# A fused attention and soft mixture of experts on one core: the dispatch softmax's second part one unit later, and the last batch's sums kept in x's unused third

## The chip, the cores and the metric

One core of a Trainium2 chip. The metric is the device time of one execution in microseconds (us); lower is better. The engines are TensorE (PE, its weight loads PEld), VectorE (DVE), ScalarE (ACT), GpSimd (POOL) and SyncE (SP), which issues all of this kernel's transfers.

## The reference

The input are q, k and v of 8 batches, 12 heads, 448 tokens and 64 columns, a matrix phi of 768 x 32, and the weights of 8 experts, w1 (768 x 1024 each) and w2 (1024 x 768 each), all fp32.

```
scores = q @ k.T / sqrt(64) - log(448)
attn   = sigmoid(scores)
x      = attn @ v                       # 3584 tokens x 768, heads side by side
logits = x @ phi                        # 3584 x 32 slots
d      = softmax of logits over the 3584 tokens (+ 1e-9 under the line)
slots  = d.T @ x                        # 32 x 768, 4 per expert
out_e  = relu(slots_e @ w1_e) @ w2_e    # for each of the 8 experts
c      = softmax of logits over the 32 slots (+ 1e-9)
result = c @ out                        # 3584 x 768
```

## The kernel before, in words

**Attention.** The heads are taken in pairs: 6 pairs per batch, 48 in all, each with its tokens in a free dimension of 448. The keys of a pair come in units of 128; the last 64 keys of two pairs share a unit, so two pairs make 7 units, a batch 21 and the whole 168 (`seq`). A unit (p, c) has two halves. `score` (L133) multiplies keys and queries into a PSUM tile `sc`, and a sigmoid on ScalarE (L137) writes the unit's buffer `att`, one of three in rotation. `weigh` (L157) multiplies that with v into `av`; it runs two units later (`LAG` = 2), so TensorE alternates between scoring unit i and weighing unit i - 2. Tile `av0` belongs to even pairs and `av1` to odd ones. The unit that two pairs share (c = 3) writes both.

After the third unit of a pair, `evac_a` (L160, VectorE) copies one half of the pair's `av` to x; after the shared unit, for an even pair, `evac_b` (L164) adds the other half. The weighing of the shared unit writes `av0` too, and it waits until `evac_a` has read it.

x is kept in `xr`, three thirds of three pairs each. A batch uses two of them, the next batch the third and the first, and so on; batch 7, the last, uses the thirds 2 and 0.

**The dispatch softmax, batch by batch.** While batch b + 1 is scored and weighed, the softmax over tokens of batch b is taken up, with a running maximum and a running sum per slot. Its parts are put into the attention's loop by three tables, `early`, `middle` and `late`, whose keys are places in that loop (i); with g the last unit of batch b, place g + n + LAG is the one at which unit g + n is weighed. In `late` what stands there follows the unit's weighing and its `evac_a` or `evac_b`.

- g + 2: `logits_job` (L173 on TensorE, then `softmax_a`: maximum and difference on VectorE), `softmax_b` (two sigmoids on ScalarE, L201 and L202, whose quotient is the exponential), then `turn` (L167, a transpose of one pair's x) and `softmax_c` (VectorE: reciprocal L207, product L208, transpose L209, sum L211 or L214, running sum L215, and the logits' transpose L217).
- g + 3 is the third unit of the next batch's first pair, so `evac_a` stands there; g + 4 is the shared unit, with `evac_b` and two turns.
- g + 5: `spread`, which SP issues: the weights go to DRAM (`zd`, L221) and come back in four copies (`dr`, L224); and two turns. g + 7: the last turn.
- g + 10: `slot_job`: the slot sums on TensorE (`slot_mm`, L246), added up in `acc` on VectorE (L261, L263).

The engines' orders are as written (`manual_schedule` for TensorE, SP, VectorE and ScalarE), each a strict sequence.

**The last batch** is not followed by attention. `last_job` does its softmax at once, on TensorE, VectorE and ScalarE, and its slot sums; L307 adds `acc`, scaled, to them in four instructions and writes `total`, 128 x 768, and L314 multiplies that into `sT`, the slots' input, on which the experts depend.

**Weights.** w1 and w2 are cut into 128 units of 384 KB. 56 go to the tiles `wa` during the attention. Of 11 further tiles `wb` the memory is that of the attention's pools `ldq`, `ldv`, `at` (where `att` is) and `xp` (where `xr` is), in this order; their loads (`load_unit`, L85) are issued after `last_job`, one after the other on SP, and each waits until what lay in its place is done with. The remaining 61 units follow in the ring of `wa` and `wb`, each when its tile's unit has been used. The experts run with w1 (L429) and then, for each half of the columns, with w2 (L528). After each half 16 output blocks are computed (L510, copied by L511) and written (L513), through the same ring and the same SP queue; those of the first half are computed within the second half's w2 steps.

Of the kernel before, what the change touches and what calls it, by code (L numbers as in the profile page):

```python
# [9 lines left out]
F32 = mybir.dt.float32  # L10
# [7 lines left out]
DM, NSLOT, E, SPE, F = 768, 32, 8, 4, 1024  # L18
P = 128
NFK = 3  # L20
LAG = 2
W_STEPS = 140
NPR = H // 2
NKC = DM // P
# [17 lines left out]
def soft_moe_attention(ctx: ExitStack, tc: tile.TileContext, qk, v, vl, phi, w1, w2, cst, out):  # L42
# [48 lines left out]
    with ExitStack() as actx:  # L91
        ldq = actx.enter_context(tc.tile_pool(name="ldq", bufs=3))
        ldv = actx.enter_context(tc.tile_pool(name="ldv", bufs=1))
        at = actx.enter_context(tc.tile_pool(name="at", bufs=3))
# [5 lines left out]
        xr = xp.tile([P, 3, 3, S], F32, name="xr")  # L100
# [4 lines left out]
        def x_of(p):  # L105
            b, hp = divmod(p, NPR)
            return xr[:, (2 * b + hp // 3) % 3, hp % 3, :]
# [58 lines left out]
        def turn(p):  # L166
            nc.vector.transpose(x_of(p), x_of(p))  # L167
# [9 lines left out]
        def logits_job(b):  # L177
            lg = ps_sc.tile([P, 2, 512], F32, name="sc")[:, 0, :]
            logits(lg, b, range(NPR))
            nc.vector.tensor_copy(lgs[0:96, :], lg[0:96, 0:P])  # L180
            nc.vector.tensor_copy(lgs[96:128, 0:64], lg[96:128, 0:64])
            softmax_a(b)
# [15 lines left out]
        def softmax_b(b):  # L198
            zt, pe = dts[b][:, 0, :], dts[b][:, 1, :]
            n = P if b == 0 else P + 1  # L200
            nc.scalar.activation(pe[:, 0:n], zt[:, 0:n], AF.Sigmoid)  # L201
            nc.scalar.activation(zt[:, 0:n], zt[:, 0:n], AF.Sigmoid, scale=-1.0)  # L202

        def softmax_c(b):
            zt, pe = dts[b][:, 0, :], dts[b][:, 1, :]
            n = P if b == 0 else P + 1
            nc.vector.reciprocal(zt[:, 0:n], zt[:, 0:n])  # L207
            nc.vector.tensor_tensor(out=pe[:, 0:n], in0=pe[:, 0:n], in1=zt[:, 0:n], op=ALU.mult)  # L208
            nc.vector.transpose(zt[:, 0:P], pe[:, 0:P])  # L209
            if b == 0:  # L210
                nc.vector.tensor_reduce(out=mz[:, 1:2], in_=pe[:, 0:P], axis=AX.X, op=ALU.add)  # L211
            else:
                zb = small.tile([P, 1], F32, name="zb")
                nc.vector.tensor_reduce(out=zb[:], in_=pe[:, 0:P], axis=AX.X, op=ALU.add)  # L214
                nc.vector.scalar_tensor_tensor(  # L215
                    out=mz[:, 1:2], in0=mz[:, 1:2], scalar=pe[:, P:P + 1], in1=zb[:], op0=ALU.mult, op1=ALU.add)
            nc.vector.transpose(lt_all[:, b, :], lgs[:])  # L217

        def spread(b):
            flat = bounce.tile([P, P], F32, name="zd")  # L220
            nc.sync.dma_start(flat[:], dts[b][:, 0, 0:P])  # L221
            drs[b] = xp.tile([P, 4, NBK * BLK], F32, name="dr")
            for a in range(4):
                nc.sync.dma_start(drs[b][32 * a:32 * a + 32, :, :], flat[:].rearrange("(j i) n -> i j n", j=4))  # L224
# [31 lines left out]
        def slot_job(b):  # L256
            sl = slot_mm(b)
            for g in range(2):
                part = sl[g][:, :, 0:NPR * BLK]
                if b == 0:  # L260
                    nc.vector.tensor_copy(acc_of(g), part)  # L261
                else:
                    nc.vector.scalar_tensor_tensor(  # L263
                        out=acc_of(g), in0=acc_of(g), scalar=dts[b][:, 1, P:P + 1], in1=part,
                        op0=ALU.mult, op1=ALU.add)

        def last_job(b, lgt):
# [33 lines left out]
            nc.vector.tensor_tensor(out=cw[:, 2:3], in0=m1[:, 1:2], in1=pa[:, P:P + 1], op=ALU.subtract)  # L301
            nc.scalar.activation(cw[:, 3:4], cw[:, 2:3], AF.Exp)
            nc.vector.tensor_scalar(sw, sel4, cw[:, 3:4], None, op0=ALU.mult)
            total = at.tile([P, DM], F32, name="att")
            by_block = total[:].rearrange("p (k a n) -> p k a n", k=NKC, a=4)
            for a in range(4):
                nc.vector.scalar_tensor_tensor(  # L307
                    out=by_block[:, :, a, :], scalar=cw[:, 1:2],
# [37 lines left out]
        for r in range(NP // 2):  # L346
            p = 2 * r
            seq += [(p, c) for c in range(NFK + 1)] + [(p + 1, c) for c in range(NFK)]
        per_b = len(seq) // B
        early, middle, late = {}, {}, {}  # L350
        for b in range(B - 1):
            g = (b + 1) * per_b - 1
            early[g + 2 + LAG] = [lambda b=b: logits_job(b)]
            middle[g + 2 + LAG] = [lambda b=b: softmax_b(b)]
            late[g + 2 + LAG] = [lambda b=b: turn(b * NPR), lambda b=b: softmax_c(b)]
            late[g + 4 + LAG] = [lambda b=b: turn(b * NPR + 1), lambda b=b: turn(b * NPR + 2)]
            late[g + 5 + LAG] = [lambda b=b: spread(b), lambda b=b: turn(b * NPR + 3), lambda b=b: turn(b * NPR + 4)]
            late[g + 7 + LAG] = [lambda b=b: turn(b * NPR + 5)]
            late[g + 10 + LAG] = [lambda b=b: slot_job(b)]

        for i in range(len(seq) + LAG):
# [20 lines left out]
            if i >= LAG:  # L382
                u = seq[i - LAG]
                weigh(u)
                p, c = u
# [13 lines left out]
        logits(lgt[:, 0, :], B - 1, [NPR - 1])  # L399
        turn(NP - 4)  # L400
        finish = last_job(B - 1, lgt)

    state["wpb"] = ctx.enter_context(tc.tile_pool(name="wpb", bufs=1, reuse_waits="tile"))
# [113 lines left out]
    for hf in range(2):  # L517
        po = ps_o.tile([P, 512], F32, name="po")
        n = 0
# [67 lines left out]
```

## Time and profile before

| | |
|---|---|
| median of 3 runs | 425.53 us (423.01 to 427.61) |
| the profiled execution | 426.35 us, of which the span from first to last instruction 424.5 us |
| busy, share of the span | PE 89%, DVE 39%, ACT 49%, POOL 1% |
| transfers | 97.64 MB, mean 230 GB/s |
| mean granted TensorE clock | 0.955 |

In the profile's rows L133 is the line of the kernel; `att<-sc` names the tile written and those read; a bracket at a row's end is the idle time of that engine just before it and what ended the idle time. `SPq` is SP's queue: its rows show the issue of a transfer, not the transfer. In the list of waits stand the total in us, the number of waits and the longest. Under `windows` the columns are each engine's busy time with its instructions, then TensorE's clock, the share of the DMA engines' time, and GB/s.

### The profile page before, as it was taken

What the parts mean: (1) busy time and instruction counts of PE and PEld (TensorE: products, weight loads), DVE (VectorE), ACT (ScalarE), POOL (GpSimd) and SP (SyncE); (2) the same over time, 40 slices, a digit from 0 to 9 for tenths busy, and PEclk for the clock granted to TensorE, in tenths of its full rate; (3) what the DMA queues carried; (4) which work ended last, traced back from release to release, by engine and by line L of the source; (5) the groups of instructions that cost most, each with busy time, mean ns of one, the idle gap of its engine ahead of it and who ended that gap; (6) DMA issues with size and microseconds to landing.
All of it is one profiled execution on the core that took longest, in us unless ns stands there. A gap on an engine that the chain in (4) does not pass through costs nothing.

```text
span 424.5 us, 11237 instructions
## 1 busy us (share of the span) xinstructions
PE 377.5 (89%) x4794; PEld 170.1 (40%) x4794; DVE 164.2 (39%) x383; ACT 206.0 (49%) x274; POOL 2.4 (1%) x12
## 2 busy tenths in 40 slices
PE   8999899989989998998999899899879968889730
PEld 5333343434334343433434343344355433334410
DVE  0222632453263236226423622542534653144430
ACT  4666546655645655564565556555400223433430
POOL 0000000000000000000000000000010000000000
PEclk9999999999999999999999999999968998969885
DMA  6667467558736755874665565252309999999987
GB/s 232 222 226 242 149 210 258 188 146 277 233 129 205 255 176 179 258 247 159 196 227 200 192 217 180 84 144 83 112 13 349 399 400 402 401 401 394 301 282 229
DMA packets 48770, 97.64 MB, mean 230 GB/s; under 512 B 5072, under 2 KB 26192, under 8 KB 48720
## 3 DMA queue, kind: packets, MB, share of 16 engines
q1 hardware_dynamic: 48720, 96.92, 67.0%
q8 instruction: 38, 0.62, 0.6%
q14 instruction: 12, 0.10, 0.1%
HBM read 85.43 MB, written 11.47 MB: 228 GB/s over the span
## 4 chain that ended last, share of the span: by engine, by line
PE 77%; DVE 10%; issue 4%; ACT 3%; DMA 1%; DVEq 0%; ACTq 0%
PE av L157 28%; PE sc L133 28%; PE po L528 5%; PE sc L173 3%; PE av L246 2%; PE sc L246 2%; PE ph L510 2%; PE ph L429 2%; DVE t L207 2%; PE pt L446 1%; DVE xr L160 1%; DVE tmp L442 1%; DMA out_dram<-wa 1%; PE pt L484 1%; PE pt L510 1%
## 5 line engine op out<-in xcount | busy, mean ns | idle before, releaser
L137 ACT ACTIVATE att<-sc,nbias 128x896 f32<-128x896 f32 x168 | 169.1, 1007 | 126.8 <-PE sc L133 126.8
L133 PE MATMUL sc<-qkt 64*64 64x448 f32 x1344 | 158.1, 541 | 0.2 <-ACT att L137 0.2
L157 PE MATMUL av<-att,v 64*64 64x448 f32 x1152 | 134.0, 536 | 0.0
L160 DVE COPY xr<-av 128x448 f32<-128x448 f32 x48 | 30.0, 625 | 135.9 <-PE av L157 135.7
L133 PEld LDWEIGHTS sc<-qkt 64*64 64x64 f32 x1344 | 50.1, 134 | 73.2 <-issue 67.1
L157 PEld LDWEIGHTS av<-att,v 64*64 64x64 f32 x1152 | 43.9, 133 | 63.9 <-issue 63.9
L164 DVE TENSOR_TENSOR xr<-xr,av 128x448 f32<-128x448 f32 x48 | 29.8, 621 | 24.2 <-PE av L157 23.4
L157 PE MATMUL av<-att,vl 64*64 64x448 f32 x192 | 23.2, 554 | 11.8 <-DVE xr L160 11.8
L167 DVE STREAM_TRANSPOSE xr<-xr 128x448 f32<-128x448 f32 x48 | 28.1, 621 | 1.1 <-PE sc L173 1.1
L429 PE MATMUL ph<-wa,sT 128*32 128x256 f32 x336 | 21.0, 400 | 0.7 <-DVE lt_all L317 0.7
L511 DVE COPY wa<-pt 96x384 f32<-96x384 f32 (+1 forms) x31 | 16.0, 552 | 7.9 <-PE pt L510 6.8
L511 ACT COPY wa<-ph 96x384 f32<-96x384 f32 (+1 forms) x31 | 13.6, 479 | 11.2 <-PE ph L510 11.0
L246 PE MATMUL sc<-xr,dr 32*32 32x192 f32 x448 | 17.7, 355 | 0.0
L510 PE MATMUL ph<-st,wb 128*128 128x384 f32 (+1 forms) x32 | 14.1, 441 | 3.6 <-DVE st L545 3.5
L246 PE MATMUL av<-xr,dr 32*32 32x192 f32 x448 | 17.4, 354 | 0.0
L157 PEld LDWEIGHTS av<-att,vl 64*64 64x64 f32 x192 | 6.4, 131 | 27.4 <-DVE xr L160 25.0
L429 PEld LDWEIGHTS ph<-wa,sT 128*32 128x32 f32 x336 | 10.4, 113 | 8.4 <-issue 1.9
L173 PE MATMUL sc<-xr,phit 128*32 128x128 f32 (+1 forms) x384 | 12.3, 262 | 1.4 <-DVE xr L164 1.4
L246 PEld LDWEIGHTS av<-xr,dr 32*32 32x32 f32 x448 | 10.8, 108 | 6.4 <-issue 5.2
L173 PEld LDWEIGHTS sc<-xr,phit 128*32 128x32 f32 x384 | 9.9, 109 | 7.8 <-issue 4.9
L510 PE MATMUL pt<-st,wb 128*128 128x384 f32 (+1 forms) x32 | 12.4, 388 | 0.0
L451 ACT COPY hh<-pt 128x32 f32<-128x32 f32 x8 | 1.5, 187 | 21.9 <-PE pt L446 21.9
(117 smaller groups left out, 194.6 us busy)
## 6 DMA issues: line engine op xcount, KB each, us to landing
wa<-in_w_dram SPq DMA_DIRECT2D x112, 384.0 KB, 7.4
qkt<-in_qk_dram SPq DMA_DIRECT2D x48, 448.0 KB, 3.6
v<-in_v_dram SPq DMA_DIRECT2D x48, 192.0 KB, 2.8
wb<-in_w_dram SPq DMA_DIRECT2D x16, 384.0 KB, 6.4
out_dram<-wa SPq DMA_DIRECT2D x15, 384.0 KB, 5.0
out_dram<-wa SPq DMA_DIRECT2D x16, 288.0 KB, 5.7
dr<-zd SPq DMA_DIRECT2D x28, 64.0 KB, 2.0
vl<-in_vl_dram SPq DMA_DIRECT2D x24, 64.0 KB, 2.6
```

The lines of the kernel that those rows point to most:

```text
L133: nc.tensor.matmul(sc[64 * t:64 * t + 64, h, 0:S], qkts[pt][r, S + k0:S + k0 + 64], qkts[pt][r, 0:S], start=True, stop=True)
L137: nc.scalar.activation(att[:], sc[:, :, 0:S], AF.Sigmoid, bias=nbias[:], scale=QSCALE)
L157: nc.tensor.matmul(o[r, t, 0:S], w, att[row, h, :], start=start, stop=stop)
L160: nc.vector.tensor_copy(x_of(p), avs[p][:, 1, 0:S])
L164: nc.vector.tensor_tensor(out=x_of(p), in0=x_of(p), in1=av[:, 0, 0:S], op=ALU.add)
L167: nc.vector.transpose(x_of(p), x_of(p))
L173: nc.tensor.matmul(lg[32 * j:32 * j + 32, 0:n], phi_sb[:, hp, :], x_of(b * NPR + hp)[:, j * P:j * P + n], start=(hp == 0), stop=(hp == NPR ...
L246: nc.tensor.matmul(sl[a // 2][32 * j:32 * j + 32, a % 2, 0:NPR * BLK], drs[b][32 * a:32 * a + 32, j, c * BLK:(c + 1) * BLK], y[32 * a:32 * ...
L429: nc.tensor.matmul(ph[32 * j:32 * j + 32, uu, :], sT[:, 3 * kh + kc, :], utile[("w1", e, 2 * uu + j // 2, kh)][:, kc * 256:(kc + 1) * 256] ...
L510: nc.tensor.matmul(pf[0:n, 0:HALF], cts[g, i][:, c0:c0 + n], st[:], start=True, stop=True)
L511: (nc.scalar.copy if j == 0 else nc.vector.tensor_copy)(ov[:, j, :], pf[0:n, 0:HALF])
L528: nc.tensor.matmul(po[32 * fl:32 * fl + 32, 0:HALF], hT[e][:, 4 * g + fl, :], ut, start=(n == 0), stop=(n == 2 * E - 1))
```

## The change

`softmax_c` is put into `late` at g + 3 instead of g + 2. `total` is a view of the first 768 columns of the middle third of `xr`, which the last batch does not use, instead of a buffer of the rotation `att`.

```diff
-            total = at.tile([P, DM], F32, name="att")
-            by_block = total[:].rearrange("p (k a n) -> p k a n", k=NKC, a=4)
+            total = xr[:, 1, 0:2, :].rearrange("p a n -> p (a n)")[:, 0:DM]
+            by_block = total.rearrange("p (k a n) -> p k a n", k=NKC, a=4)
...
-            late[g + 2 + LAG] = [lambda b=b: turn(b * NPR), lambda b=b: softmax_c(b)]
+            late[g + 2 + LAG] = [lambda b=b: turn(b * NPR)]
+            late[g + 3 + LAG] = [lambda b=b: softmax_c(b)]
```

On VectorE, at the dispatch softmax of batch 0 (`t_474` is its softmax tile; the other six batches read alike), the order before and now:

```order
 L195 TENSOR_SCALAR t_474<-lgs,mz 128x128 [waits DVE_49]
 L167 STREAM_TRANSPOSE xr<-xr 128x448
+L160 COPY xr<-av_442 128x448 [waits PE_49]
 L207 RECIPROCAL t_474<-t_474 128x128 [waits Activation_49]
 L208 TENSOR_TENSOR t_474<-t_474 128x128 [waits DVE_49]
...
 L211 TENSOR_REDUCE mz<-t_474 128x1
 L217 STREAM_TRANSPOSE lt_all<-lgs 128x128
-L160 COPY xr<-av_442 128x448 [waits PE_49]
-L164 TENSOR_TENSOR xr<-xr,av_442 128x448 [waits DVE_49,PE_49]
+L164 TENSOR_TENSOR xr<-xr,av_442 128x448 [waits PE_49]
```

The copy L160 (`evac_a`) now stands ahead of `softmax_c`'s instructions, which come between it and L164 (`evac_b`).

On SP, the third to eleventh of the `wb` loads before the change, with the semaphores that each waits for (DMAHW: an earlier transfer's landing):

```order
L85 DMA wb_3434<-in_w_dram 128x768 [waits DMAHW7_49]
L85 DMA wb_3436<-in_w_dram 128x768 [waits DMAHW2_49]
L85 DMA wb_3438<-in_w_dram 128x768 [waits DMAHW3_49,DVE_49,DMAHW4_49,PE_49,Activation_49]
L85 DMA wb_3440<-in_w_dram 128x768 [waits Activation_49]
L85 DMA wb_3442<-in_w_dram 128x768
L85 DMA wb_3444<-in_w_dram 128x768
L85 DMA wb_3446<-in_w_dram 128x768 [waits DMAHW5_49]
L85 DMA wb_3448<-in_w_dram 128x768 [waits DMAHW6_49]
L85 DMA wb_3450<-in_w_dram 128x768 [waits DMAHW7_49]
```

and now:

```order
L85 DMA wb_3433<-in_w_dram 128x768 [waits DMAHW7_49]
L85 DMA wb_3435<-in_w_dram 128x768 [waits DMAHW2_49]
L85 DMA wb_3437<-in_w_dram 128x768 [waits DMAHW3_49,DMAHW4_49,PE_49,Activation_49]
L85 DMA wb_3439<-in_w_dram 128x768 [waits Activation_49]
L85 DMA wb_3441<-in_w_dram 128x768
L85 DMA wb_3443<-in_w_dram 128x768
L85 DMA wb_3445<-in_w_dram 128x768 [waits DMAHW5_49,DVE_49,PE_49]
L85 DMA wb_3447<-in_w_dram 128x768 [waits DMAHW6_49]
L85 DMA wb_3449<-in_w_dram 128x768 [waits DMAHW7_49]
```

The wait for VectorE has moved from the fifth load to the ninth. The value that the fifth load waits for on TensorE was that of the last L314 matmul and is now that of the last L157 matmul; the wait for L314 is on the ninth.

## The prediction

> **What bounds the kernel now.** I read the page first: where the engines and the transfers are full.
>
> ```profile
> span 424.5 us, 11237 instructions
> PE   8999899989989998998999899899879968889730
> ...
> PEclk9999999999999999999999999999968998969885
> DMA  6667467558736755874665565252309999999987
> GB/s 232 222 226 242 149 210 258 188 146 277 233 129 205 255 176 179 258 247 159 196 227 200 192 217 180 84 144 83 112 13 349 399 400 402 401 401 394 301 282 229
> ```
>
> There are two regimes. In the first 28 slices (10.6 us each, so up to 297 us) TensorE is full at full clock and the transfers are half busy. From slice 31 (318 us) on, the DMA engines are full, at 400 GB/s while weights are read and under 300 when outputs are written, and TensorE is not. Between them lies slice 30 with 13 GB/s: a hole in which nothing is moved. So in the first regime only idle time of TensorE counts, in the second only bytes moved later than need be. The list of waits tells who makes either wait:
>
> ```profile
> PE av L157 <- DVE xr L160: 11.8, 7, 1.7
> ...
> SPq L85 <- DMA wa<-in_w_dram: 32.2, 53, 1.3
> ...
> SPq L85 <- DVE att L307: 13.7, 1, 13.7
> ...
> SPq L85 <- PE av L314: 1.6, 1, 1.6
> ```
>
> The first row is nearly all the idle time that TensorE has in the attention: 7 waits, one per batch whose dispatch softmax runs there, 11.8 us together. The third and fourth are one load of weights that SP holds for 13.7 us until the last batch's sums (L307) are written and for 1.6 us more until TensorE has read them (L314); everything on SP stands behind it. The second row shows what follows: 53 loads that each wait for an earlier load's landing, so the queue is full from there on. Both of the change's parts lie exactly on these rows.
>
> **Part one: softmax_c behind evac_a.** The timeline at batch 6's softmax:
>
> ```profile
> 271.46 0.93 PE L157 MATMUL av<-att,v 64*64 64x448 f32 x8
> 271.87 0.97 DVE L207 RECIPROCAL t<-t 128x129 f32<-128x129 f32 x1 [0.55 <-ACT t L202]
> 272.21 0.93 PE L133 MATMUL sc<-qkt 64*64 64x448 f32 x8
> 272.87 0.29 DVE L208 TENSOR_TENSOR t<-t 128x129 f32<-128x129 f32 x1
> 273.20 0.31 DVE L209 STREAM_TRANSPOSE t<-t 128x128 f32<-128x128 f32 x1
> ...
> 273.85 0.31 DVE L217 STREAM_TRANSPOSE lt_all<-lgs 128x128 f32<-128x128 f32 x1
> 274.19 0.62 DVE L160 COPY xr<-av 128x448 f32<-128x448 f32 x1
> 274.87 0.98 PE L157 MATMUL av<-att,vl 64*64 64x448 f32 x8 [1.73 <-DVE xr L160]
> ```
>
> TensorE ends the third unit's weighing at 272.39 (271.46 + 0.93). Its copy out of PSUM (L160) could start then, but VectorE is in softmax_c, which starts at 271.87 and ends at 274.16: 2.3 us. The copy runs 274.19 to 274.81, and the fourth unit's weighing, which writes the same tile, starts at 274.87 after 1.73 us of idle TensorE. An ordinary round shows what is left without softmax_c:
>
> ```profile
> 297.50 0.93 PE L133 MATMUL sc<-qkt 64*64 64x448 f32 x8
> 297.75 0.62 DVE L160 COPY xr<-av 128x448 f32<-128x448 f32 x1 [3.23 <-PE av L157]
> 298.43 0.98 PE L157 MATMUL av<-att,vl 64*64 64x448 f32 x8
> ```
>
> The copy starts 0.25 us into the scoring and the weighing follows 0.93 us after the scoring began, with no gap. With the change the boundary has this form: copy 272.42 to 273.04, weighing at 272.21 + 0.93 = 273.14, 1.73 us earlier. The same instructions stand at all seven, so the row's 11.8 us are gone, and no more, since the rest of the attention has no wait on TensorE to win.
>
> The stall moves onto what stands behind softmax_c on VectorE, and these rows price it:
>
> ```profile
> 275.89 0.62 DVE L164 TENSOR_TENSOR xr<-xr,av 128x448 f32<-128x448 f32 x1 [1.07 <-PE av L157]
> 276.42 2.22 DVE L167 STREAM_TRANSPOSE xr<-xr 128x448 f32<-128x448 f32 x4
> 280.43 0.62 DVE L160 COPY xr<-av 128x448 f32<-128x448 f32 x1 [1.79 <-PE av L157]
> ...
> 276.67 0.33 SPq L112 DMA_DIRECT2D qkt<-in_qk_dram  x1
> 277.04 0.43 SPq L221 DMA_DIRECT2D zd<-t  x1
> 280.26 2.85 SPq L224 DMA_DIRECT2D dr<-zd  x4
> ...
> 284.80 0.39 PE L246 MATMUL av<-xr,dr 32*32 32x192 f32 x8
> ```
>
> softmax_c now runs 273.06 to 275.36, so evac_b (L164), which could start at 274.15, starts at 275.37 and ends at 275.99, then four transposes to 278.2. The next copy (L160) is wanted at 280.43 - 1.73 = 278.70. The 1.79 us of idle VectorE before it shrink to 0.5: tight, but nothing is late. evac_b itself is late by 1.2 us; it frees the tile for weighing that comes four units (6 us) later, so nobody waits.
>
> The second follower is SP. The bounce of the softmax weights (L221) needs the transpose L209, which ended at 273.51 and now ends at 273.06 + 1.64 = 274.70. SP reaches L221 after the load before it, which waits for scoring on TensorE, so it moves with TensorE: 277.04 - 1.73 = 275.31. The margin is 0.6 us, so the issue is not late. But the trip has no room behind it: the fourth copy of `dr` is issued about 282.7, such copies take this long,
>
> ```profile
> dr<-zd SPq DMA_DIRECT2D x28, 64.0 KB, 2.0
> ```
>
> so it lands about when the slot sums start (284.80). If the trip took longer because loads stand 1.7 us closer, TensorE would wait there instead. Bounds: no loss (trip unchanged), or, as batch 6 stands so near, half of the gain given back over the seven, 5.9 us. The transfers are half busy there and the trip keeps its distance to TensorE's work, so I go near the first and take 0.4 us lost in all. Part one: -11.8 + 0.4 = **-11.4 us**, between -5.9 and -11.8.
>
> **Part two: the sums in x's unused third.** What the held load waits for:
>
> ```profile
> 301.07 16.17 SPq L85 DMA_DIRECT2D wb<-in_w_dram  x2
> 302.07 1.73 PE L157 MATMUL av<-att,v 64*64 64x448 f32 x16
> ...
> 313.81 0.74 DVE L307 SCALAR_TENSOR_TENSOR att<-acc,cw,av 128x192 f32<-128x192 f32 x2 [3.73 <-PE av L246]
> 315.34 1.50 PE L314 MATMUL av<-t,att 128*128 128x32 f32 x12 [1.32 <-DVE att L307]
> ```
>
> The fourth `wb` load goes at 301.07; the row's 16.17 us are two issues, and the second, the fifth load, goes at 316.9, when L314 has ended (316.84). With `total` out of the sigmoid buffers the fifth needs only the last weighing (303.80), and so do the sixth to eighth; the ninth lies under x and is the one that waits for L314. So four loads move from behind 316.9 into the hole, which they fill from 303.9 to about 308. Nothing else moves data there (the 13 GB/s), and VectorE, ScalarE and TensorE work on tiles that are long in SBUF, so I find no loss. One load is 384 KB = 393 kB, at 401 GB/s 0.98 us; four are **3.9 us** by which the full queue behind 316.9 runs earlier.
>
> The Trainium skill ("DMA: Bandwidth & Descriptors", Where 436 GB/s comes from) puts the HBM limit of one core near 358 GB/s, by which four loads would be 4.4 us; this trace's 399 to 402 GB/s say otherwise, and the trace is used.
>
> Does the end get it all? No matmul waits for these weights (no such row among the waits), so the gain passes only through the queue's order to the outputs.
>
> ```profile
> 398.38 0.85 ACT L511 COPY wa<-ph 128x384 f32<-128x384 f32 x2 [1.72 <-PE ph L510]
> 398.55 2.08 DVE L511 COPY wa<-pt 128x384 f32<-128x384 f32 x4 [0.71 <-DMA out_dram<-wa]
> ...
> 401.11 18.98 SPq L513 DMA_DIRECT2D out_dram<-wa  x16
> ...
> 398.00:424.00 26.00, 8.54 (x32) 5.48 (x32) 8.25 (x16) 7.04 (x16) 0.00 (x0) 0.66 0.86 266
> ```
>
> The second half's first output is complete in SBUF at about 399.1, and is the first of the last 16 that SP issues, at 401.11. Moved by 3.9 it would go at 397.2, which is before its data exist; it goes at 399.1, still with some 2 us of earlier outputs in flight. I take off 0.3 for engines that run dry: **-3.6 us**, between 0 (below, first rival) and -3.9.
>
> **Sum.** Against the profiled execution: 426.35 - 11.4 - 3.6 = 411.35. The median of the three runs is 0.8 lower than that execution (425.53), so **410.5 us**. The new address costs L307 and L314 nothing: same shapes, same order, same waits.
>
> **Rivals.**
> - *The tail's gain does not reach the end* (0.13). The second half's outputs are then set by TensorE's path, not by the queue. For: the 2 us of cover above, and TensorE's clock in the tail, which falls to 6 and 5 tenths in single slices. With one more half-clock slice there (digit 6: 0.4 x 10.6 us of clock lost, about 4 us of matmul at full rate, half of it on the path) the outputs come 2 us later and the cover is gone; two cost all. Against: the DMA share stays near 9 to the end. Time: 426.35 - 11.4 - 0.8 = 414.1. The Trainium skill ("TensorE: Matmul & The Clock Gate", Part 1) says the clock is judged in free-running windows of 3.4 us, so where the half-clock stretches fall differs from run to run; the three times (423.01 to 427.61) would agree, but no row here shows it.
> - *The bounce binds* (0.06): the `dr` copies land late and half of part one's gain is given back at the slot sums. For: batch 6's rows above. Against: no wait of L246 for a transfer stands in the list of waits now, and nothing of the trip starts later against TensorE. Time: 426.35 - 5.9 - 3.6 - 0.8 = 416.0.
> - *The change doesn't do what it says* (0.03): the copy still finds VectorE busy, or the weighing waits for evac_b too (then it starts at about 276.0 rather than 274.87), and the fifth load is held by another tile in that memory. Time near 425.
> - *Slower* (0.02): SP reaches L221 before L209, which is now late, and the `dr` copies, the v load and the qk load behind them all slip; TensorE then waits at the slot sums. It decides from 15.0 / 7 = 2.1 us per boundary on; with 3 us, 425.5 - 15.0 + 21 = 431.5. Against: the 0.6 us of margin; L209 would have to be over 2.7 us later than worked out.
>
> **How the numbers follow.** The forecast has 0.76. Its own bounds: both parts whole and luck with the clock, 426.35 - 0.8 - 11.8 - 3.9 - 2.1 (that half of a slice's lost clock) = 407.8; runs of one kernel spread by about 2 us either way, so 407.0. Upward the range takes in the first rival, 414.1, to 414.5; the bounce and the last two rivals are outside. 1% is 4.3 us, about what a measurement of this kernel can tell: forecast and the first two rivals are faster by more (0.95), the third is no change (0.03), the last slower (0.02).
>
> **What would show it.** In the changed profile: the row of L157's waits for L160 on TensorE gone, or under 1 us; L207 right behind L160 and L164 0.02 us behind L217; one batch's period shorter by 1.6 to 1.7 us; four `wb` loads issued at about 292 to 294 (303.9 - 11.4), and SP's wait for L307 still there on the ninth; from there to the end about 3.6 us less than the 107.6 from 316.9 now. Waits of TensorE on L246 of more than 1 us in all, or a last slot sum that starts less than 10 us before its present time, would make part one wrong; an unchanged distance from L314's end to the end of the span would make part two wrong.

## The result, and the profile after

| | before | changed |
|---|---|---|
| median, same chip | 426.25 us (423.01 to 427.61, 4 runs) | 411.4 us (407.73 to 413.59, 4 runs) |
| ratio | | 0.9685, 95% interval 0.9626 to 0.9744 |
| profiled execution, its span | 426.35 us, 424.5 us | 413.59 us, 411.8 us |

The change makes the kernel 3.1% faster [2.6% to 3.7%], about 13.4 us. Here and below a ratio and its interval come from the undisturbed executions and are not the quotient of the two medians, which is 0.9652 here (14.9 us) and lies inside the interval.

The changed kernel's page, the rows shown of before:

```profile
span 411.8 us, 11229 instructions
PE   8999999999999999999999999999879878889720
PEclk9999999999999999999999999999969998999875
DMA  6677567658756755866765584342719999999896
GB/s 239 211 235 247 168 224 228 210 161 292 235 175 206 237 177 195 296 220 187 241 216 179 182 269 139 97 156 67 239 62 358 402 400 403 400 401 373 277 290 194
```

The hole is narrower: slice 29 now moves 239 GB/s and slice 30 moves 62, where before they moved 112 and 13. From slice 31 on the picture is the old one: about 400 GB/s for weights, then under 300 for outputs.

The changed kernel's list of waits (us in all, how many, the longest), first TensorE's largest rows:

```profile
PE pt L447 <- DVE tmp L443: 5.9, 7, 3.2
PE ph L511 <- DVE st L546: 3.5, 2, 1.7
```

and of the same list SP's rows:

```profile
SPq L85 <- DMA wa<-in_w_dram: 32.2, 53, 1.4
SPq L224 <- DMA zd<-t: 25.5, 7, 4.9
SPq L85 <- DVE xr L307: 9.8, 1, 9.8
...
SPq L85 <- PE av L157: 2.3, 1, 2.3
...
SPq L85 <- PE av L314: 1.6, 1, 1.6
```

The row of 11.8 us that headed TensorE's list is gone; what heads it now stands in the tail and stood there before. On SP one load is still held for L307 and L314, now the ninth, and for 9.8 us instead of 13.7, since SP first waits 2.3 us for the last weighing (the row of L157) and then issues four loads ahead of it. A row that nobody looked for has grown: the wait for `zd` to land, 25.5 us over seven batches with a longest of 4.9. In the kernel before it reads:

```profile
SPq L224 <- DMA zd<-t: 21.0, 7, 3.9
```

Batch 6's softmax in the changed kernel's timeline (start, duration):

```profile
262.78 0.93 PE L157 MATMUL av<-att,v 64*64 64x448 f32 x8
263.53 0.93 PE L133 MATMUL sc<-qkt 64*64 64x448 f32 x8
263.78 0.62 DVE L160 COPY xr<-av 128x448 f32<-128x448 f32 x1 [1.13 <-PE av L157]
264.32 0.95 DVE L207 RECIPROCAL t<-t 128x129 f32<-128x129 f32 x1
264.46 0.98 PE L157 MATMUL av<-att,vl 64*64 64x448 f32 x8
265.64 0.31 DVE L209 STREAM_TRANSPOSE t<-t 128x128 f32<-128x128 f32 x1
266.29 0.30 DVE L217 STREAM_TRANSPOSE lt_all<-lgs 128x128 f32<-128x128 f32 x1
266.52 0.58 DVE L164 TENSOR_TENSOR xr<-xr,av 128x448 f32<-128x448 f32 x1
266.63 0.42 SPq L221 DMA_DIRECT2D zd<-t  x1
```

The copy starts 0.25 us into the scoring and the weighing 0.93 us after the scoring began (263.53 to 264.46), as in an ordinary round. L207 follows L160, L164 follows L217, and `zd` is issued 0.68 us after L209 ends (265.95), so it is not held.

The loads after `last_job` on SP, in two stretches of the timeline:

```profile
293.50 13.54 SPq L85 DMA_DIRECT2D wb<-in_w_dram  x5
...
306.72 1.76 SPq L85 DMA_DIRECT2D wb<-in_w_dram  x3
```

The first row begins with the fifth load. Its five issues are the fifth to the eighth, at 293.50, 293.87, 294.36 and 294.83, and the ninth, which is held until L314 has ended (306.69); hence the 13.54 us.

### The profile page after: what moved, and what is told of

It is laid out like the page before. It is cut to its first block, busy times and chain, and to the rows that moved or that the text cites. A ratio compares the mean times of both kernels' runs of the same rounds, so it can differ in the third digit from the quotient of the medians.

```text
span 411.8 us, 11229 instructions
## 1 busy us (share of the span) xinstructions
PE 375.9 (91%) x4794; PEld 170.3 (41%) x4794; DVE 162.5 (39%) x383; ACT 205.8 (50%) x274; POOL 2.4 (1%) x12
## 4 chain that ended last, share of the span: by engine, by line
PE 85%; DVE 6%; issue 3%; ACT 2%; DVEq 0%; ACTq 0%
PE av L157 32%; PE sc L133 31%; PE po L529 4%; PE sc L173 3%; PE av L246 2%; PE sc L246 2%; PE ph L430 2%; PE ph L511 2%; PE pt L447 1%; DVE tmp L443 1%; PE pt L511 1%; PE pt L485 1%; PE av L341 1%; DVE wa L512 1%; PE av L279 1%
## 5 line engine op out<-in xcount | busy, mean ns | idle before, releaser
L133 PE MATMUL sc<-qkt 64*64 64x448 f32 x1344 | 159.7, 540 | 0.4 <-ACT att L137 0.4
L157 PE MATMUL av<-att,v 64*64 64x448 f32 x1152 | 135.6, 536 | 0.0
L160 DVE COPY xr<-av 128x448 f32<-128x448 f32 x48 | 30.0, 625 | 137.4 <-PE av L157 137.4
L133 PEld LDWEIGHTS sc<-qkt 64*64 64x64 f32 x1344 | 50.9, 133 | 72.6 <-issue 66.5
L157 PEld LDWEIGHTS av<-att,v 64*64 64x64 f32 x1152 | 44.7, 133 | 63.9 <-issue 63.9
L164 DVE TENSOR_TENSOR xr<-xr,av 128x448 f32<-128x448 f32 x48 | 29.5, 615 | 16.4 <-PE av L157 15.6
L157 PE MATMUL av<-att,vl 64*64 64x448 f32 x192 | 23.2, 554 | 0.0
L430 PE MATMUL ph<-wa,sT 128*32 128x256 f32 x336 | 20.9, 399 | 0.7 <-DVE lt_all L317 0.7
L512 ACT COPY wa<-ph 96x384 f32<-96x384 f32 (+1 forms) x31 | 13.7, 478 | 9.0 <-PE ph L511 8.7
L246 PE MATMUL av<-xr,dr 32*32 32x192 f32 x448 | 18.0, 354 | 0.0
L246 PE MATMUL sc<-xr,dr 32*32 32x192 f32 x448 | 17.8, 352 | 0.0
L430 PEld LDWEIGHTS ph<-wa,sT 128*32 128x32 f32 x336 | 10.5, 114 | 8.2 <-issue 1.8
L173 PE MATMUL sc<-xr,phit 128*32 128x128 f32 (+1 forms) x384 | 12.3, 262 | 1.4 <-DVE xr L164 1.4
L246 PEld LDWEIGHTS av<-xr,dr 32*32 32x32 f32 x448 | 10.5, 108 | 6.5 <-issue 5.2
L173 PEld LDWEIGHTS sc<-xr,phit 128*32 128x32 f32 x384 | 9.9, 109 | 7.8 <-issue 4.9
L157 PEld LDWEIGHTS av<-att,vl 64*64 64x64 f32 x192 | 6.5, 131 | 15.4 <-DVE xr L160 13.1
```

What stands on the lines that cost most here:

```text
L133: nc.tensor.matmul(sc[64 * t:64 * t + 64, h, 0:S], qkts[pt][r, S + k0:S + k0 + 64], qkts[pt][r, 0:S], start=True, stop=True)
L157: nc.tensor.matmul(o[r, t, 0:S], w, att[row, h, :], start=start, stop=stop)
L160: nc.vector.tensor_copy(x_of(p), avs[p][:, 1, 0:S])
L164: nc.vector.tensor_tensor(out=x_of(p), in0=x_of(p), in1=av[:, 0, 0:S], op=ALU.add)
L173: nc.tensor.matmul(lg[32 * j:32 * j + 32, 0:n], phi_sb[:, hp, :], x_of(b * NPR + hp)[:, j * P:j * P + n], start=(hp == 0), stop=(hp == NPR ...
L246: nc.tensor.matmul(sl[a // 2][32 * j:32 * j + 32, a % 2, 0:NPR * BLK], drs[b][32 * a:32 * a + 32, j, c * BLK:(c + 1) * BLK], y[32 * a:32 * ...
```

## The experiments

The main theory is that of the prediction: part one removes TensorE's wait, and part two lets the full queue of transfers run four loads earlier to the end. Its rivals: the tail's gain does not reach the end, or the bounce of the softmax weights takes part of the gain back. Twelve runs follow, in three groups of four; each group has its own 11 runs of the kernel before, and the groups ran on different chips.

| group (before) | kernel | median us | ratio, 95% interval |
|---|---|---|---|
| 1 (425.1) | part1_only | 414.01 | 0.9736 [0.9696, 0.9776] |
| 1 | part2_only | 421.0 | 0.9893 [0.9845, 0.9942] |
| 1 | after_again | 408.88 | 0.9629 [0.9588, 0.9669] |
| 1 | sums_in_acc | 411.23 | 0.9624 [0.9563, 0.9684] |
| 2 (424.44) | spread_earlier | 407.97 | 0.9626 [0.9590, 0.9661] |
| 2 | c_two_later | 409.88 | 0.9669 [0.9635, 0.9702] |
| 2 | keep_warm | 411.81 | 0.9715 [0.9672, 0.9757] |
| 2 | spread_warm | 408.81 | 0.9646 [0.9602, 0.9691] |
| 3 (423.05) | after_third | 408.2 | 0.9664 [0.9615, 0.9712] |
| 3 | spread_again | 408.48 | 0.964 [0.9605, 0.9675] |
| 3 | second_half_only | 408.11 | 0.9649 [0.961, 0.9688] |
| 3 | all_three | 409.24 | 0.967 [0.9634, 0.9705] |

### Each part alone

part1_only is the kernel before with only the new place of `softmax_c`; part2_only has only the new place of `total`; after_again is the changed kernel once more.

```diff
 # part1_only, against the changed kernel
-            total = xr[:, 1, 0:2, :].rearrange("p a n -> p (a n)")[:, 0:DM]
-            by_block = total.rearrange("p (k a n) -> p k a n", k=NKC, a=4)
+            total = at.tile([P, DM], F32, name="att")
+            by_block = total[:].rearrange("p (k a n) -> p k a n", k=NKC, a=4)
 # part2_only, against the changed kernel
-            late[g + 2 + LAG] = [lambda b=b: turn(b * NPR)]
-            late[g + 3 + LAG] = [lambda b=b: softmax_c(b)]
+            late[g + 2 + LAG] = [lambda b=b: turn(b * NPR), lambda b=b: softmax_c(b)]
```

> softmax_c one unit later, but the last batch's sums still in a sigmoid buffer. Theory: the part is worth the seven waits of the weighing for evac_a (11.8 us in the trace of before) less what the slot sums wait longer for the bounced weights (1.2 us in the trace of the changed kernel), about 10.4 us: 426.25 - 10.4 = 415.9, ratio 0.976. SP still holds the fifth wb load for L307 for over 12 us, and from the end of L314 to the end of the span it takes 107 to 108 us as before. Rival, that the tail alone made the gain differ (the seven gaps were worth less, the tail more): 418 or above.

> The last batch's sums in x's unused third, but softmax_c where it was. Theory: four loads move into the hole, the last weight load lands 3.9 to 4.2 us earlier after L314 than before, and the end comes 2.6 to 3.6 us earlier: 422.7 to 423.7, ratio 0.9915 to 0.994. The 11.8 us of waits stay. Rival, that the tail's gain does not reach the end: within 1 us of before, ratio over 0.997, though the last load lands earlier.

> The changed kernel once more, for a second profile of it. Theory: the last 16 outputs took 18.9 us in its first profile against 16.8 before by chance of that execution (it was the slowest of four, 413.59 against a median of 411.4); a second profile shows 16.5 to 18 us for them and 103.5 to 104.5 us from the end of L314 to the end of the span. Rival, that the change itself makes the outputs slower: 18.5 us or more again.

Against 425.1 us, part one is worth 11.2 us [9.5 to 12.9] and part two 4.5 us [2.5 to 6.6]. They add: 0.9736 x 0.9893 = 0.9632, and both together gave 0.9629. In part1_only's profile the end stands 105.4 us behind L314, not the 107 to 108 that were expected, although the last weights land as late as before; the table of ends below shows how far single executions scatter. From the first to the last landing of the final 16 outputs it took 16.4 us in after_again and 19.2 in after_third, 18.9 in the changed kernel's first profile and 16.8 before: they scatter, and no slowing by the change is shown. The waits of part1_only, first on TensorE, then on SP:

```profile
PE pt L447 <- DVE tmp L443: 5.9, 7, 3.2
...
SPq L85 <- DVE att L307: 13.8, 1, 13.8
```

and of part2_only:

```profile
PE av L157 <- DVE xr L160: 11.8, 7, 1.7
...
SPq L85 <- DVE xr L307: 7.2, 1, 7.2
```

Each part removes its own wait and leaves the other's. That part two alone is faster, with an interval that stays below 1, speaks against the rival by which the tail's gain does not reach the end.

### Where part one lost a little: the bounce

From the first L173 matmul of batch 0 to that of the last batch the kernel before took 258.93 us and the changed one 248.68, 247.96 and 247.78 in its three profiled executions: 10.3 to 11.2 us less, not 11.8. Most of the seven stalls are won whole or nearly so; the largest part of what is missing stands at batch 5's slot sums. On TensorE's matmul rows no wait is seen there. Its weight loads show it (the changed kernel):

```profile
237.49 0.18 PEld L246 LDWEIGHTS av<-xr,dr 32*32 32x32 f32 x8 [0.74 <-issue]
237.93 0.15 PEld L246 LDWEIGHTS av<-xr,dr 32*32 32x32 f32 x8 [0.25 <-DMA dr<-zd]
238.41 0.18 PEld L246 LDWEIGHTS sc<-xr,dr 32*32 32x32 f32 x8 [0.34 <-issue]
238.93 0.13 PEld L246 LDWEIGHTS sc<-xr,dr 32*32 32x32 f32 x5 [0.33 <-DMA dr<-zd]
```

Four groups of matmuls each start when one of the four `dr` copies lands (237.39, 237.88, 238.31 and 238.89). The slot sums last 3.08 us to the next scoring instead of 2.12. Over the seven batches they last 1.39 us longer than 7 x 2.12, and 1.09 and 0.90 in the changed kernel's other two profiles, against about 0.2 before.

Two kernels try the cause from both sides. spread_earlier issues the bounce one unit earlier; c_two_later moves `softmax_c` one unit further, behind `evac_b`, so that the bounce is issued later.

```diff
 # spread_earlier
-            late[g + 4 + LAG] = [lambda b=b: turn(b * NPR + 1), lambda b=b: turn(b * NPR + 2)]
-            late[g + 5 + LAG] = [lambda b=b: spread(b), lambda b=b: turn(b * NPR + 3), lambda b=b: turn(b * NPR + 4)]
+            late[g + 4 + LAG] = [lambda b=b: spread(b), lambda b=b: turn(b * NPR + 1), lambda b=b: turn(b * NPR + 2)]
+            late[g + 5 + LAG] = [lambda b=b: turn(b * NPR + 3), lambda b=b: turn(b * NPR + 4)]
 # c_two_later
-            late[g + 3 + LAG] = [lambda b=b: softmax_c(b)]
-            late[g + 4 + LAG] = [lambda b=b: turn(b * NPR + 1), lambda b=b: turn(b * NPR + 2)]
+            late[g + 4 + LAG] = [lambda b=b: softmax_c(b), lambda b=b: turn(b * NPR + 1), lambda b=b: turn(b * NPR + 2)]
```

> As the changed kernel, but the bounce of the softmax weights is issued one unit earlier, ahead of the qk and w loads that stood before it on SP. Theory, that the slot sums wait for the bounce since the change (1.2 us over the seven batches in its first profile, most at batch 5): the slot sums take 2.1 to 2.2 us at all seven and the kernel is 1.0 to 1.3 us faster than the changed one, ratio about 0.960 against 0.963. Rival, that the 1.2 us are something else on TensorE (its clock, or matmul order): batch 5 still takes 2.9 to 3.1 us and the time stays.

> softmax_c two units later than before the change instead of one, so that it stands behind evac_b too. Theory: nothing waits for evac_b, so that order gains nothing, but the transpose that the bounce needs ends 1.7 to 1.9 us later, the bounce is issued about 1.1 us later, and the slot sums wait about 1 us more at six of seven batches: 5 to 7 us slower than the changed kernel, ratio 0.975 to 0.979. Rival, that the bounce has room: no change against the changed kernel, 0.963.

SP's queue at batch 5, first in the changed kernel:

```profile
229.32 0.33 SPq L112 DMA_DIRECT2D qkt<-in_qk_dram  x1
229.70 0.42 SPq L85 DMA_DIRECT2D wa<-in_w_dram  x1
230.22 0.38 SPq L221 DMA_DIRECT2D zd<-t  x1
235.59 1.75 SPq L224 DMA_DIRECT2D dr<-zd  x4
```

in spread_earlier:

```profile
227.41 0.33 SPq L124 DMA_DIRECT2D vl<-in_vl_dram  x1
227.86 0.35 SPq L221 DMA_DIRECT2D zd<-t  x1
229.50 2.48 SPq L224 DMA_DIRECT2D dr<-zd  x4
232.07 0.38 SPq L112 DMA_DIRECT2D qkt<-in_qk_dram  x1
```

and in c_two_later:

```profile
229.72 0.33 SPq L112 DMA_DIRECT2D qkt<-in_qk_dram  x1
230.10 0.42 SPq L85 DMA_DIRECT2D wa<-in_w_dram  x1
231.14 0.33 SPq L221 DMA_DIRECT2D zd<-t  x1
236.08 1.75 SPq L224 DMA_DIRECT2D dr<-zd  x4
```

The `dr` copies are issued as soon as `zd` has landed, so the row of L224 dates that landing. With the landings from the transfers' own records:

| batch 5 | zd issued | zd landed | its trip | last dr landed | slot sums begin | they last |
|---|---|---|---|---|---|---|
| before | 239.92 | 243.63 | 3.7 | 246.89 | 247.15 | 2.12 |
| changed | 230.22 | 235.57 | 5.4 | 238.89 | 237.52 | 3.08 |
| c_two_later | 231.14 | 236.07 | 4.9 | 239.37 | 238.06 | 3.02 |
| spread_earlier | 227.86 | 229.48 | 1.6 | 233.51 | 236.28 | 2.12 |

Two things make up the trip. The first is what stands ahead of `zd` in the queue. Of the 98 trips in the fourteen profiles (seven batches each) 91 end 0.15 to 0.39 us after the load issued just ahead of `zd` has landed. At batch 5 that is a load of weights (384 KB) behind one of q and k (448 KB); spread_earlier issues `zd` ahead of both, and the trip falls to 1.6 us. At batches 0 to 4 its trips are longer, 2.0 to 3.4 us, but they end early enough. The Trainium skill ("DMA: Bandwidth & Descriptors", HWDGE ordering) says that each DMA engine takes its descriptors in the order of its ring and that a transfer's signal lands only after that engine's earlier writes; these trips agree with it.

The second is not the queue's. Before the change the same two loads stand ahead of `zd` at batch 5, and the trip is 3.7 us and not 5.4. In the changed kernel 120 of the 128 packets of `zd` start from 232.62 to 233.29, and the last eight, a sixteenth of the transfer, only from 234.50 on. Between the two, all the transfers of 233.4 to 234.5 us are three packets, one of them of 16 KB on another queue:

```profile
DMA packets 3, 0.02 MB, mean 18 GB/s; under 512 B 1, under 2 KB 1, under 8 KB 2
q8 instruction: 1, 0.02, 5.4%
```

By its kind it carries instructions, and it runs from 233.57 to 234.52. In after_again, after_third, part1_only and c_two_later the last eight packets at batch 5 wait in the same way, and start within 0.02 us of the end of such a packet; these are the five profiles in which batch 5's slot sums last longest, 2.83 to 3.08 us. second_half_only, whose attention is the changed kernel's, has such a packet at batch 5 too, but none of `zd`'s packets wait behind it: its trip is 3.8 us and its slot sums last 2.13. So most of batch 5's extra time is the instruction packet's doing, and the earlier bounce helps because it leaves room for it: in all_three the packet holds `zd` at batch 5 to a trip of 3.5 us, and nothing waits. Why it holds `zd` in some executions and not in others is not shown; nor are the smaller excesses at other batches (0.3 us at batch 2 of the changed kernel) taken apart.

So c_two_later costs next to nothing, far less than a late issue was expected to: `zd` is issued 0.92 us later at batch 5 and lands 0.50 later, behind the instruction packet both times. Its 0.9669 lies within the changed kernel's three results (0.9629, 0.9664, 0.9685), though above spread_earlier's 0.9626 of the same group. In spread_earlier, spread_again, spread_warm and all_three no wait of L246 for `dr` is left. In spread_again each of the first six batches takes 35.92 us (in spread_earlier the first takes 36.35), and from first to last it takes 246.94 us: 12.0 us less than before, the whole of it.

That this is worth time at the end is not settled:

> The changed kernel a third time, beside the next kernels on one chip: ratio 0.961 to 0.968. In its profile the slot sums wait 0.8 to 1.4 us in all beyond 2.12 us each, and from L314's end to the end of the span it takes 103 to 105.5 us.

> The bounce one unit earlier, a second time, beside the changed kernel on the same chip. Theory: 1.0 to 1.4 us faster than it (the wait of the slot sums gone, the tail the same), so 0.9965 to 0.9975 of it. Rival, that the gain in the attention is lost in the tail, whose end the outputs set: the same time, though the last slot sums stand 1.0 to 1.4 us earlier.

Side by side, 0.9664 and 0.964: 1.0 us for the earlier bounce by the ratios, with intervals that overlap for the most part, while the medians (408.2 and 408.48) stand the other way. The attention of that execution is 0.8 us shorter than after_third's.

### The ninth load

`total` in `xr` still makes the ninth load wait for L307 and L314, since `wb` lies under `xr` too. sums_in_acc keeps the sums in `acc` itself, in the order of the blocks:

```diff
+        acc_by_block = acc[:].rearrange("p (k a n) -> p k a n", k=NKC, a=4)
-            for g in range(2):
-                part = sl[g][:, :, 0:NPR * BLK]
+            for a in range(4):
+                part = sl[a // 2][:, a % 2, 0:NPR * BLK].rearrange("p (k n) -> p k n", k=NKC)
...
-                    out=by_block[:, :, a, :], scalar=cw[:, 1:2],
-                    in0=acc[:, a * NPR * BLK:(a + 1) * NPR * BLK].rearrange("p (k n) -> p k n", k=NKC),
+                    out=acc_by_block[:, :, a, :], scalar=cw[:, 1:2], in0=acc_by_block[:, :, a, :],
...
-                    ps[:, kc * NSLOT:(kc + 1) * NSLOT], total[:, kc * P:(kc + 1) * P], sw, start=True, stop=True)
+                    ps[:, kc * NSLOT:(kc + 1) * NSLOT], acc[:, kc * P:(kc + 1) * P], sw, start=True, stop=True)
```

> As the changed kernel, but the last batch's sums are written over acc, whose layout is made that of the sums (so that the slot sums are added up by four instructions per batch instead of two, off the chain), and the ninth wb load waits for the last slot sums only. The ninth load then goes about 3.0 us earlier against L314's end, and all behind it. Theory that the transfer queue bounds the tail to the end: 2.5 to 3.0 us faster than the changed kernel, ratio about 0.962. Rival, that the second half's outputs are now ready too late: they are complete only 0.8 us before they are issued in the changed kernel, so at most 0.8 us is gained, ratio 0.9665 or more, and the DMA share falls below 0.9 just before the second half's outputs.

0.9624 against 0.9629 of after_again: nothing gained. SP's wait for L307 is gone, but another has grown, first as it reads in the changed kernel, then in sums_in_acc:

```profile
SPq L85 <- PE ph L430: 4.3, 12, 0.8
...
SPq L85 <- PE ph L426: 7.9, 13, 3.7
```

The ninth load goes at 301.96, some 3 us before L314's end, and then SP waits for the experts' first products (L426 is the w1 matmul there, L430 in the changed kernel): the loads behind it go to tiles whose w1 units are not yet used. The last load lands only 1.2 us earlier against L314's end (66.6 instead of 67.8), and keep_warm and spread_earlier, which leave these loads as they are, come to 66.4 and 66.5; so the three loads' lead of some 3 us has not reached the last load. The end does not move: 103.9 us after L314's in its profile, as in after_again's.

### What bounds the end now

Everything from L314's end, in us, in one profiled execution each:

| | last weights landed | second half's first output ready | end of span | last weights to last output |
|---|---|---|---|---|
| before | 71.95 | 82.27 | 107.7 | 34.7 |
| part1_only | 71.85 | 82.12 | 105.4 | 32.5 |
| part2_only | 67.39 | 77.95 | 103.1 | 34.7 |
| changed | 67.75 | 79.3 | 105.1 | 36.3 |
| after_again | 67.79 | 82.26 | 103.9 | 35.1 |
| after_third | 67.51 | 79.23 | 105.7 | 37.2 |
| keep_warm | 66.4 | 78.28 | 102.0 | 34.6 |
| second_half_only | 67.55 | 82.41 | 104.4 | |

Part two brings the weights' end 4.2 to 4.6 us forward in part2_only and the changed kernel's three profiles (some 5.5 in keep_warm). The outputs then take 32.5 to 37.2 us in kernels that write the same bytes, so a single execution's end cannot be read to better than 2 or 3 us. The changed kernel's profiled executions (413.59, 411.14 and 412.32 us) were also among the slower of theirs. The second column has two levels, 78 to 79 and 82: in the executions of the second a stretch of 6.8 us at half clock falls in the first half's end. The end does not follow it: the changed kernel's earliest end, 103.9, has the late level and its other two the early one. Two kernels ask which of the two, the queue or TensorE, holds the end. keep_warm gives TensorE matmuls on an unused tile in its idle moments of the tail; they add nothing to the output. second_half_only empties the queue.

```diff
 # keep_warm
+    def warm2(n):
+        pd = ps_t.tile([P, 512], F32, name="pt")
+        for _ in range(n):
+            nc.tensor.matmul(pd[:, 0:P], ident, ident, start=True, stop=True)
 # second_half_only
+            if hf == 1:
             nc.sync.dma_start(
```

The helper is called with 12 before the last `h_part`, with 4 after the copy of `so` and with 7 after the `pr` matmul; the page counts 68 more matmuls. spread_warm is spread_earlier with keep_warm's edit; all_three is that with sums_in_acc's as well.

> As the changed kernel, with 12 idle matmuls (128 x 128 by 128, result unused) ahead of the last expert's transposes and 4 and 7 of them in the two waits of TensorE between the halves. Theory, that the times of one kernel spread because an idle window puts TensorE at half clock for 6.8 us around the first half's end in some executions (second half's outputs ready 82.1 to 82.5 us after L314's end with that stretch, 78.0 to 79.3 without): the stretch is gone in the profile, ready at 78 to 79.5, mean clocks of all executions 0.97 or more, and the median 1 to 2.5 us below the changed kernel, ratio about 0.958. Rival, that the drain of the outputs sets the end whichever way: clock up, ready earlier, time as the changed kernel, 0.961 to 0.965.

> Both of these: the bounce one unit earlier and the idle matmuls. If the two theories hold, the gains add: 2 to 3.5 us below the changed kernel, ratio about 0.955. If only the bounce's does, 0.960; if neither, 0.963.

> As the changed kernel, but the first half's outputs are computed and not written (the first 384 columns of the result are missing), so that no earlier output is in flight when the second half's begin. Theory that the queue of outputs sets the end: it comes 3 us or more earlier against L314's end than the changed kernel's 103.9 to 105.1. Rival, that by now the moment at which the second half's outputs are ready sets it: they are ready 79 to 82.3 us after L314's end as now, the 16 of them take 18 to 19 us and 2 us of latency, and the end comes 100 to 103.5 us after L314's end, at most 2 us earlier for the same readiness.

> The bounce one unit earlier, the idle matmuls and the sums in acc together, so that loads, readiness and slot sums are all early at once. Theory, that queue and readiness bound the tail alike, so that either alone gained nothing: 2 to 4 us faster than the changed kernel, ratio 0.953 to 0.958. Rival, that the outputs' own rate sets the end: ratio 0.960 to 0.964.

The clock in 40 slices, in after_again:

```profile
PEclk9999999999999999999999999999968998969985
```

and in keep_warm:

```profile
PEclk9999999999999999999999999999968999999985
```

The dip in the 36th slice is gone and the first output of the second half is ready at 78.3 instead of 82.3. One pair of profiles does not show that the extra matmuls did it, since the changed kernel's other two profiles are without the dip as well (79.3 and 79.2). But none of the three profiles with these matmuls has it, and six of the eleven without them do. The mean clock of keep_warm's six executions was 0.961 to 0.981, where 0.97 or more was expected of all. The time is not better for it: 0.9715 where the changed kernel had 0.9629 to 0.9685, and with the earlier bounce 0.9646 against 0.9626 of the same group without the extra matmuls. So readiness alone does not hold the end. second_half_only's transfers in 40 slices:

```profile
DMA  6677477658656756776667675352549999992096
GB/s 241 200 247 249 151 217 253 199 180 293 213 174 187 259 195 201 237 243 215 186 221 244 201 232 151 118 160 76 170 144 351 401 399 403 400 402 87 23 303 217
```

and its last outputs on SP's timeline:

```profile
385.64 17.61 SPq L515 DMA_DIRECT2D out_dram<-wa  x16
```

With 16 outputs unwritten the queue lies nearly idle in slices 37 and 38 (87 and 23 GB/s), and yet the kernel takes 0.9649 of the time before, not told apart from the changed kernel's 0.9664 of the same group: its first output goes at 385.64, when it is ready, and the remaining 16 need 21 us. So the queue alone does not hold the end either. Two paths that now end at about the same time would fit both results, but this is argued and not shown: all_three, which was to shorten both, gave 0.967 [0.9634, 0.9705] where that theory expected 0.953 to 0.958. It is not a clean refutation either, since its last weights landed only 0.3 to 0.6 us earlier than the changed kernel's (67.2 behind L314's end).

What sets the time of the outputs (32.5 to 37.2 us) stays open, but the transfers' own records show one part of it. The outputs go in packets of 1536 bytes, which take 76 to 79 ns each, and the weights in packets of 3072 bytes, which take 125 ns. From these an estimate for 16 engines without a pause is 311 to 323 GB/s for outputs and 393 for weights. second_half_only's sixteen outputs alone kept the engines busy for 17.3 us of the 19.7 in which their packets ran, so even a free queue leaves little to win between the first output and the last. Whether it is the size of the packets or their being writes is not told apart.

The fastest versions, spread_earlier and spread_again (0.9626 and 0.964), are not told apart from the change itself.

## Why the prediction was right

**Part one, -11.4 us: measured -11.2 [-12.9 to -9.5] in part1_only.** The whole row of seven waits is gone, and the boundary has the form that was worked out, down to the 0.93 us. The new neighbours were right as well: `evac_b` comes late and nobody waits for it, and `zd` is issued 0.68 us after L209, where a margin of 0.6 was worked out. Batch periods fell from 37.65 to between 35.92 and 36.28 us, except that of batch 5 (36.94).

The weak step is the sentence "the trip keeps its distance to TensorE's work". At batch 6, from which it was reasoned, it held: 3.3 us after and 3.2 before. At batch 5 the trip became 5.4 us instead of 3.7, and the 0.4 us that were taken off measure 0.7 to 1.2 in the three profiles (0.90 to 1.39, less 0.2). The side from which trouble was expected, the issue's margin, did not matter. Nor did the trip of batch 5 grow because loads stand 1.7 us closer, the reason that the prediction named: a packet of instructions held the last eight packets of `zd`. The rival by which the bounce takes back 5.9 us was right in kind and about five to eight times too large.

**Part two, -3.6 us: measured -4.5 [-6.6 to -2.5] in part2_only.** The four loads went into the hole at 293.50 to 294.83, where about 292 to 294 was said; the ninth is still held; the last weights land 4.2 us earlier where 3.9 was worked out. No row gave the 0.3 that were taken off for engines that run dry, and no run tells it from nothing. The sign that was named for the profile, an end about 3.6 us nearer to L314, gives 2.6 (107.7 to 105.1) and in the other two executions 3.8 and 2.0. It was a poor sign, since the outputs' time varies by more than that; the times are the better evidence.

**The first rival** (the tail's gain does not reach the end) falls by part2_only. But the cover of 2 us that it spoke of is indeed smaller: the first of the last 16 outputs went 2.0 us after it was ready before, and 1.4, 0.1 and 0.4 us in the changed kernel's profiles. Behind the change neither sums_in_acc nor second_half_only got a further gain out of the queue.

**Sum.** 410.5 was predicted. The changed kernel's medians are 411.4, 408.88 and 408.2 in three sets of runs, with before at 426.25, 425.1 and 423.05. The mechanism of both parts was right; that the first median lies within 1 us of the sum is partly luck, since the loss to the bounce and the gain of part two were both put too small, which cancel, and the three medians themselves spread by 3.2 us.

## What to carry to other kernels

A stall at the head of a strict engine order is often worth its row in the list of waits, if what is moved behind has a reader far enough away; price the next reader on every queue. A small transfer through DRAM lands when what stands ahead of it has landed: issue it before the large loads, leave room behind it for a stray packet, and look for its wait on the weight loads rather than on the matmuls. When a trip is longer than its queue explains, look at the single packets: most may be done, and a few held by another queue. When one wait is taken off and the next one gives nothing, shorten each of the remaining paths by itself before adding more; a change that shortens two of them at once tells little if it gives nothing.

## What the runs showed of the hardware

- A 64 KB write to DRAM lands 0.15 to 0.39 us after the load issued just ahead of it on the same queue, in 91 of 98 cases. At batch 5 it took 1.6 us ahead of two loads of 448 and 384 KB (3.5 in all_three, where a packet of instructions held it), and 3.4 to 5.4 us behind them.
- A 16 KB packet of the kind `instruction`, about 0.9 us long, can hold a sixteenth of such a write: in five profiles the last eight of 128 packets started within 0.02 us of its end, and the write landed 1.5 to 1.6 us after the load ahead of it.
- Outputs leave at 266 to 332 GB/s in full slices of the profiles of before, the changed kernel and its two parts, where loads come at 400. Packets of 1536 bytes took 76 to 79 ns there, the loads' packets of 3072 bytes 125 ns. The outputs' total time varies by 4.7 us between executions of like kernels.
- Stretches of half clock fall in the tail of some executions and not of others: after_again has one from 360.8 to 367.6 us. But for the last of each execution, all of them in the fourteen profiles last 3.4, 6.8 or 13.7 us. The Trainium skill ("TensorE: Matmul & The Clock Gate", Part 1) says that the clock is judged in free-running windows of 3.4 us; the trace agrees, with stretches of one, two and four such windows. With the 68 small matmuls of keep_warm the stretch of 6.8 us in the first half's end was absent, in three profiles of three; without them it was there in six of eleven.
